# Table activations in earlier gaps, the first row block evacuated in halves, DMA transposes for half of the second batch, and the first cast emitted earlier in a fused retention and Fourier-mix kernel

## The chip, the cores and the metric

One core of a Trainium2 chip. The metric is the device time of one execution in microseconds (us), lower is better. The times are medians of several executions; the profile is of one execution, and its span is a little shorter than the time of the same run (252.5 us of 254.16).

## The reference, cut to what matters

```python
# attention: B, H, S, D = 4, 8, 768, 64; a decaying state per head
state = gamma * state + k[t] (x) v[t]
y[t]  = scale * q[t] @ state
# mix and feed-forward: x = y as [B, S, 512]
mixed = real(fft(fft(x, axis=1), axis=2))
u  = x + mixed
un = (u - mean(u)) / sqrt(var(u) + 1e-6)
out = u + relu(un @ w_ch1) @ w_ch2          # 512 -> 2048 -> 512
```

## The kernel before

Per batch the kernel works on four pairs of heads. A pair's q and k are cast to fp16 (`q16z`, `kd`), transposed (`qTz`, `kT`), multiplied (`wkA`, masked to `atm`), combined with the running state (`s`) to `wkY`, and written to `x`. Then the two Fourier transforms are matmuls with cosine and sine tables: folds `xab` and `eo`, first stage `ps` to `g`, second stage `pq` to `u`. Row blocks `kb` 0 to 5 of 128 rows each are centred (`un`), transposed (`unT`) and fed to the hidden layer `psh` and the output layer `psc`. Batches overlap: while batch b runs its two layers, batch b+1 runs its attention. Only the first batch has nothing to overlap with; this stretch of some 36 us is called the head. `filler(n)` issues n matmuls on zeros whose results nobody reads.

```python
def csn_unit(c):                      # one of the tables; three of them
    nc.scalar.activation(csn[:, c, :], rs[2 * c + 1][:, 0:384], AF.Sin, ...)
...
# end of the first batch's list of units (the head)
un += a(3) + e(3, (0, 0), (1, 0)) + [kv0_unit(3), filler(4), sc_unit(3), t_act(4, 2),
                                     csn_unit(0), csn_unit(1), csn_unit(2)]
un += e(3, (0, 1), (1, 1))
un += [yx_unit(3), yi_unit(3, 0), x0_unit(3, 0), filler(2), yi_unit(3, 1), x0_unit(3, 1), ...]
...
# rows: normalise, then transpose
def norm_unit(b, kb):
    ...
    if b == 0 and kb < 3:
        una = nc.scalar.activation(un, u[:, kb, :], AF.Identity,
                                   bias=fd[0]["mu"][:, kb:kb + 1], scale=-1.0)
...
def unT_unit(b, kb):
    if b >= NPE:                      # NPE = 2: batches 2 and 3 by DMA
        nc.sync.dma_start_transpose(unT[:, :, kb * P:(kb + 1) * P], un)
        return
    for cb in range(4):               # batches 0 and 1 by TensorE
        nc.tensor.transpose(pst[:, cb, :], un[:, cb * P:(cb + 1) * P], ident16)
    ...                               # copied by DVE or ACT
...
# one pair of batches 2 and 3: casts on ACT (q) and POOL (k, v), transposes by DMA
nc.sync.dma_start_transpose(qT..., q16_of[b, i]...)
nc.sync.dma_start_transpose(kT, kd_of[b, i]...)
...
# where each unit is put, in units of a batch; the build then orders every engine's work
streams.append(([load_unit(b + 1, i) for i in range(4)], b + -0.249, b + 0.044))
ts = [0.040, 0.044] + [0.044 + 0.550 * sum(n[:j]) / sum(n) for j in range(6)]
streams.append((steps[0], b + ts[0], b + ts[1]))      # steps[0]: cast and transposes of pair 0
```

Plain loads, output stores and all DMA transposes are issued by one engine, SP, in the order that the build gives them.

## Time and profile before

| | before |
|---|---|
| median time (4 runs) | 254.38 us (254.28 to 254.48) |
| TensorE busy in the profile | 237.9 of 252.5 us |
| start of the dense hidden-layer stream | 41.65 us |
| TensorE idle, 97 to 117 us and 151 to 175 us | 0.85 and 0.81 us |

How to read it: TensorE is the engine with the most work. So outside the head a change is worth what it takes out of TensorE's work or its gaps, and inside the head what it takes out of the chain of waits. The lines stand in the prediction below.

### The profile page before, as it was taken

Reading aid. Unit: us, or ns where it says so; the run is one execution under the profiler, and the core shown is the slowest. Engines: PE = TensorE matmul, PEld = TensorE weight load, DVE = VectorE, ACT = ScalarE, POOL = GpSimd, SP = SyncE. Lnnn points to the kernel's source line nnn. Section 1 sums busy time; section 2 is a strip of 40 time slices with the busy share of each in tenths; the row PEclk is TensorE's granted clock in tenths of the full one; section 3 lists DMA queues with packets and bytes.
Section 4 is the critical chain, followed back from the end, with each engine's and each line's share of the span. In section 5 each row is a group of like instructions: output and inputs, shape, how many; then the busy total and the mean of one; then the engine's idle time right before and its main releaser. Section 6 shows DMA issues by size and latency. Waiting matters only on the chain.

```text
span 252.5 us, 5283 instructions
## 1 busy us (share of the span) xinstructions
PE 237.9 (94%) x2040; PEld 147.7 (59%) x2040; DVE 176.1 (70%) x430; ACT 124.9 (49%) x259; POOL 73.1 (29%) x129
## 2 busy tenths in 40 slices
PE   6798899999999999899999999989999999999994
PEld 2454678856776545566566546755676455545553
DVE  7989857888998786898686727987776545323211
ACT  7878768482674336873245405851156208303400
POOL 6667500494500074480001605720003105000000
PEclk9999999999999999999999999999999999999999
DMA  8999999799999169999999383594100531221012
GB/s 173 262 254 144 194 200 193 166 256 233 287 223 213 48 128 246 179 208 191 241 254 178 73 138 80 97 148 104 56 29 0 65 124 23 44 83 42 1 44 83
DMA packets 97577, 36.00 MB, mean 143 GB/s; under 512 B 88208, under 2 KB 94608, under 8 KB 97552
## 3 DMA queue, kind: packets, MB, share of 16 engines
q1 hardware_dynamic: 93328, 31.47, 62.3%
q0 software_dynamic: 4224, 4.19, 10.4%
q8 instruction: 16, 0.26, 0.4%
q14 instruction: 9, 0.07, 0.1%
HBM read 27.26 MB, written 6.29 MB: 133 GB/s over the span
## 4 chain that ended last, share of the span: by engine, by line
PE 68%; DVE 11%; ACT 7%; DMA 6%; POOL 3%; SPq 2%; issue 2%; ACTq 0%; DVEq 0%
PE psc L900 29%; PE psh L857 21%; PE psh L874 3%; PE ps L687 3%; DMA k<-in_k_dram 2%; PE wkA L568 2%; DMA kT<-kd 2%; DMA qTz<-q16z 2%; SPq L154 2%; DVE atm L570 1%; PE pq L776 1%; PE wkY L621 1%; PE pq L772 1%; ACT un L815 1%; PE wkY L617 1%
## 5 line engine op out<-in xcount | busy, mean ns | idle before, releaser
L900 PE MATMUL psc<-w,ht 128*128 128x512 f16 (+1 forms) x400 | 89.3, 370 | 0.0
L857 PE MATMUL psh<-unT,w 128*128 128x384 f16 x448 | 82.0, 326 | 0.3 <-ACT ht L861 0.3
L900 PEld LDWEIGHTS <-ht 128*128 128x128 f16 x400 | 38.1, 98 | 35.5
L857 PEld LDWEIGHTS <-w 128*128 128x128 f16 x448 | 42.9, 98 | 24.1 <-issue 0.7
L861 ACT ACTIVATE ht<-psh 128x384 f16<-128x384 f32 x73 | 34.4, 489 | 32.2 <-PE psh L857 31.3
L795 POOL TENSOR_TENSOR u<-u,x 128x256 f32<-128x256 f32 x21 | 13.4, 637 | 116.1 <-DVE u L788 111.3
L904 DVE SCALAR_TENSOR_TENSOR ob<-psc,stats,u 128x512 f32<-128x512 f32 (+1 forms) x25 | 18.2, 726 | 26.4 <-PE psc L900 26.4
L863 DVE TENSOR_SCALAR ht<-psh 128x384 f16<-128x384 f32 x39 | 21.4, 552 | 10.1 <-PE psh L857 9.7
L570 DVE TENSOR_TENSOR atm<-wkA,maskp 128x512 f16<-128x512 f32 x36 | 23.7, 684 | 2.1 <-PE wkA L568 2.0
L629 ACT ACTIVATE x<-wkY,gexp 128x384 f16<-128x384 f32 x24 | 12.7, 581 | 20.6 <-PE wkY L621 20.5
L815 ACT ACTIVATE un<-u,stats 128x512 f16<-128x512 f32 x21 | 15.1, 721 | 14.5 <-DVE stats L814 8.6
L813 DVE BATCH_NORM_STATS2 bst<-u 128x6 f32<-128x512 f32 x21 | 14.6, 694 | 10.6 <-POOL u L797 10.5
L785 ACT COPY qn<-pq 128x255 f32<-128x255 f32 x24 | 8.9, 370 | 20.1 <-PE pq L776 19.6
L596 DVE SCALAR_TENSOR_TENSOR s<-s,gkrow,wkK 128x128 f16<-128x128 f16 x48 | 16.3, 340 | 1.2
L140 PE MATMUL wps<-ht 128*128 128x512 f16 x44 | 13.6, 415 | 2.2 <-POOL ht L186 2.2
L568 PE MATMUL wkA<-qTz,kT 128*128 128x256 f16 x72 | 13.1, 273 | 1.7 <-DMA kT<-kd 0.8
L351 POOL TENSOR_SCALAR kd<-k,gexp 128x384 f16<-128x384 f32 x24 | 13.8, 586 | 2.8 <-DMA k<-in_k_dram 2.7
L797 POOL TENSOR_TENSOR u<-u,x 128x256 f32<-128x256 f32 x21 | 13.3, 636 | 2.5 <-DVE u L790 1.3
L788 DVE SCALAR_TENSOR_TENSOR u<-pq,g,qn 128x257 f32<-128x257 f32 x24 | 11.4, 475 | 3.7 <-ACT qn L785 3.6
L874 PE MATMUL psh<-unT,w 128*128 128x128 f16 x192 | 11.4, 219 | 0.4 <-ACT unT L848 0.2
L874 PEld LDWEIGHTS <-w 128*128 128x128 f16 x192 | 11.0, 98 | 0.8 <-issue 0.7
L790 DVE SCALAR_TENSOR_TENSOR u<-pq,g,qn 128x255 f32<-128x255 f32 x24 | 11.3, 469 | 0.0
(142 smaller groups left out, 306.5 us busy)
## 6 DMA issues: line engine op xcount, KB each, us to landing
q<-in_q_dram SPq DMA_DIRECT2D x16, 384.0 KB, 6.3
k<-in_k_dram SPq DMA_DIRECT2D x16, 384.0 KB, 5.7
v<-in_v_dram SPq DMA_DIRECT2D x16, 384.0 KB, 6.1
out_dram<-ob SPq DMA_DIRECT2D x23, 256.0 KB, 2.2
w<-in_moe_w_ch_dram POOLq DMA_DIRECT2D x8, 512.0 KB, 10.9
out_dram<-ob SPq DMA_DIRECT2D x2, 128.0 KB, 1.7
unT<-un SPq DMA_TRANSPOSE x12, 2.5
qTz<-q16z SPq DMA_TRANSPOSE x8, 4.6
```

What stands on the lines that cost most here:

```text
L351: kc = nc.gpsimd.tensor_scalar(out=kd[:, :, h2, :], in0=k32[:, h2], scalar1=gkd[:, h0 + h2:h0 + h2 + 1], scalar2=1.0, op0=ALU.mult, op1=AL ...
L568: nc.tensor.matmul(wk[:, c2], st["kT"][:, c, :], st["qT"][:, :, c, :], start=True, stop=True)
L570: nc.vector.tensor_tensor(out=st["atm"][:, 2 * part:2 * part + 2], in0=wk, in1=maskp[:, PAIR_ORDER[i]].unsqueeze(1).to_broadcast([P, 2, 2, ...
L596: nc.vector.scalar_tensor_tensor(out=s16[:, c], in0=s16[:, c - 1], scalar=gkrow[:, hp, 1:2], in1=wk[:, c - c0], op0=ALU.mult, op1=ALU.add)
L813: nc.vector.bn_stats(bst, u[:, kb, :])
L815: una = nc.scalar.activation(un, u[:, kb, :], AF.Identity, bias=stats[:, kb, 0:1], scale=-1.0)
L857: nc.tensor.matmul(psh, w116[:, cb, fb * P:(fb + 1) * P], unT[:, cb, rt * 384:(rt + 1) * 384], start=(cb == 0), stop=(cb == 3))
L861: nc.scalar.activation(ht16[:, fb, :], psh, AF.Relu, bias=0.0, scale=-1.0)
L863: nc.vector.tensor_scalar(out=ht16[:, fb, :], in0=psh, scalar1=-1.0, scalar2=0.0, op0=ALU.mult, op1=ALU.max)
L874: mm = nc.tensor.matmul(psh[:, f], w116[:, cb, fb * P:(fb + 1) * P], unT[:, cb, kb * P:(kb + 1) * P], start=(cb == 0), stop=(cb == 3))
L900: nc.tensor.matmul(psc[:, c0:c1], ht16[:, fb, rb3 * P:(rb3 + 1) * P], w216[:, fb, c0:c1], start=(fb == 0), stop=(fb == NFB - 1))
L904: nc.vector.scalar_tensor_tensor(out=ob[:, c0:c1], in0=psc[:, c0:c1], scalar=lb[b]["st"][:, rb, 3:4], in1=lb[b]["u"][:, rb, c0:c1], op0=AL ...
```

## The change

The intent has four parts: (1) the three `csn` activations leave the chain for gaps of ACT some 6 to 11 us earlier, and the head's last units change order, with four fillers fewer; (2) the first row block is centred and evacuated in halves; (3) row blocks 3 to 5 of the second batch (b = 1) are transposed by DMA; (4) the first pair of batches 2 and 3 is cast sooner, and their loads are put later. The diff, cut to its core:

```diff
-                una = nc.scalar.activation(un, u[:, kb, :], AF.Identity, ...)
+                for c0, c1 in (((0, 256), (256, DM)) if kb == 0 else ((0, DM),)):
+                    una = nc.scalar.activation(un[:, c0:c1], u[:, kb, c0:c1], AF.Identity, ...)
...
-            if b >= NPE:
+            if b > 1 or b and kb >= 3:
                 nc.sync.dma_start_transpose(unT[:, :, kb * P:(kb + 1) * P], un)
...
+            if b == 0 and kb == 0:
+                nc.scalar.copy(unT[:, 0:2, 0:P], pst[:, 0:2])
+                nc.scalar.copy(unT[:, 2:4, 0:P], pst[:, 2:4])
...
-        un += a(1) + [filler(1), kv0_unit(1)] + ...
+        un += a(1) + [csn_unit(0), filler(1), kv0_unit(1)] + ...
...                          (csn_unit(1) after te_unit(2, 0), csn_unit(2) after t_act(3, 2))
-        un += [fold_s(0, 0, 130, 1, 2), fold_d(0, 0, (0,)), s1_unit(0, 0, 0),
-               fold_s(0, 130, 258, 1, 2), fold_d(0, 0, (1,)), fold_d(0, 1, (0,)), px_unit(0),
-               ...  s1_unit(0, 1, 1), px_unit(1), filler(1), g0_unit(0, (2,)), mean_unit(0)]
-        un += [s2_unit(0, 0), s2_unit(0, 1), norm_unit(0, 0), ..., filler(4), unT_unit(0, 0), ...
+        un += [fold_s(0, 0, 130, 1, 2), fold_d(0, 0), s1_unit(0, 0, 0), fold_s(0, 130, 258, 1, 2),
+               px_unit(0), fold_d(0, 1, (0,)), ... s1_unit(0, 1, 1), g0_unit(0, (2,)),
+               mean_unit(0)]
+        un += [s2_unit(0, 0), px_unit(1), s2_unit(0, 1), norm_unit(0, 0), ..., filler(2), unT_unit(0, 0), ...
...
-    streams.append(([load_unit(b + 1, i) for i in range(4)], b + -0.249, b + 0.044))
+    streams.append(([load_unit(b + 1, i) for i in range(4)], b + -0.249, b + 0.152))
-    ts = [0.040, 0.044] + [...]
+    ts = [-0.040, -0.020] + [...]
```

More of the change, by code (lines that the diff above doesn't have):

```diff
@@ L808, in run @@
             if b == 0 and kb < 3:
-                una = nc.scalar.activation(un, u[:, kb, :], AF.Identity,
-                                           bias=fd[0]["mu"][:, kb:kb + 1], scale=-1.0)
+                for c0, c1 in (((0, 256), (256, DM)) if kb == 0 else ((0, DM),)):
+                    una = nc.scalar.activation(un[:, c0:c1], u[:, kb, c0:c1], AF.Identity,
+                                               bias=fd[0]["mu"][:, kb:kb + 1], scale=-1.0)
                 lb[b]["bst", kb] = bst
@@ L844, in run @@
                 nc.tensor.transpose(pst[:, cb, :], un[:, cb * P:(cb + 1) * P], ident16)
-            if (kb % 2 == 0) != (b == 0 and kb < 3):
+            if b == 0 and kb == 0:
+                nc.scalar.copy(unT[:, 0:2, 0:P], pst[:, 0:2])
+                nc.scalar.copy(unT[:, 2:4, 0:P], pst[:, 2:4])
+            elif (kb % 2 == 0) != (b == 0 and kb < 3):
                 nc.vector.tensor_copy(unT[:, :, kb * P:(kb + 1) * P], pst)
@@ L980, in first_units @@
                                                                      half_ids]
-        un += a(1) + [filler(1), kv0_unit(1)] + e(1, *std) + [sc_unit(1)]
-        un += [q0_unit(2), t0_unit(2, 0), te_unit(2, 0), filler(3), k0_unit(2), t0_unit(2, 1),
-               te_unit(2, 1)]
+        un += a(1) + [csn_unit(0), filler(1), kv0_unit(1)] + e(1, *std) + [sc_unit(1)]
+        un += [q0_unit(2), t0_unit(2, 0), te_unit(2, 0), csn_unit(1), filler(3), k0_unit(2),
+               t0_unit(2, 1), te_unit(2, 1)]
         un += y(1) + [td_dve(0), td_dve(1), yx_unit(1), filler(2)] + x(1) + [
             gk_unit(o[2]), t_act(3, 0), t_act(3, 1), v0_unit(2)]
-        un += a(2) + [filler(1), kv0_unit(2)] + e(2, *std) + [sc_unit(2), t_act(3, 2)]
+        un += a(2) + [filler(1), kv0_unit(2)] + e(2, *std) + [sc_unit(2), t_act(3, 2),
+                                                              csn_unit(2)]
         un += [q0_unit(3), w1_unit(0), t0_unit(3, 0), te_unit(3, 0), filler(3)] + y(2)
@@ L991, in first_units @@
         un += [w1_unit(g) for g in range(1, 4)] + [w2_unit(g) for g in range(4)]
-        un += a(3) + e(3, (0, 0), (1, 0)) + [kv0_unit(3), filler(4), sc_unit(3), t_act(4, 2),
-                                             csn_unit(0), csn_unit(1), csn_unit(2)]
+        un += a(3) + e(3, (0, 0), (1, 0)) + [kv0_unit(3), filler(4), sc_unit(3), t_act(4, 2)]
         un += e(3, (0, 1), (1, 1))
-        un += [yx_unit(3), yi_unit(3, 0), x0_unit(3, 0), filler(2), yi_unit(3, 1), x0_unit(3, 1),
+        un += [yx_unit(3), yi_unit(3, 0), x0_unit(3, 0), filler(1), yi_unit(3, 1), x0_unit(3, 1),
                g0_unit(0, (1,)), filler(1)]
-        un += [fold_s(0, 0, 130, 1, 2), fold_d(0, 0, (0,)), s1_unit(0, 0, 0),
-               fold_s(0, 130, 258, 1, 2), fold_d(0, 0, (1,)), fold_d(0, 1, (0,)), px_unit(0),
-               xmean_unit(0), fold_d(0, 1, (1,)), s1_unit(0, 1, 0), s1_unit(0, 0, 1),
-               s1_unit(0, 1, 1), px_unit(1), filler(1), g0_unit(0, (2,)), mean_unit(0)]
-        un += [s2_unit(0, 0), s2_unit(0, 1), norm_unit(0, 0), gr_unit(0), gr_unit(1),
-               px_unit(2), filler(4), unT_unit(0, 0), xmean_unit(1), mean_unit(1),
+        un += [fold_s(0, 0, 130, 1, 2), fold_d(0, 0), s1_unit(0, 0, 0), fold_s(0, 130, 258, 1, 2),
+               px_unit(0), fold_d(0, 1, (0,)), xmean_unit(0), fold_d(0, 1, (1,)),
+               s1_unit(0, 1, 0), s1_unit(0, 0, 1), s1_unit(0, 1, 1), g0_unit(0, (2,)),
+               mean_unit(0)]
+        un += [s2_unit(0, 0), px_unit(1), s2_unit(0, 1), norm_unit(0, 0), gr_unit(0), gr_unit(1),
+               px_unit(2), filler(2), unT_unit(0, 0), xmean_unit(1), mean_unit(1),
                norm_unit(0, 1), s2_unit(0, 2), xmean_unit(2), mean_unit(2), norm_unit(0, 2),
@@ L1056 @@
             else:
-                streams.append(([load_unit(b + 1, i) for i in range(4)], b + -0.249, b + 0.044))
+                streams.append(([load_unit(b + 1, i) for i in range(4)], b + -0.249, b + 0.152))
                 n = [len(u) for u in steps[1:]]
-                ts = [0.040, 0.044] + [0.044 + 0.550 * sum(n[:j]) / sum(n)
+                ts = [-0.040, -0.020] + [0.044 + 0.550 * sum(n[:j]) / sum(n)
                                          for j in range(6)]
```

## The prediction

> **What bounds the kernel now.** I read the page first, then the busy time by stretch, then TensorE's own order of time, then the chain that ended last, and last the DMA issues. The page says that TensorE (PE) is busy 237.9 of 252.5 us, so the first question is where the other 14.6 us lie. The busy times by stretch answer it (columns: stretch, then the busy us of PE, PEld, DVE, ACT and POOL with instruction counts, the granted clock, the DMA share and GB/s):
>
> ```profile
> 34.00:42.00 8.00, 7.13 (x99) 5.83 (x97) 5.31 (x17) 6.84 (x21) 0.26 (x4) 1.00 1.23 202
> 42.00:62.00 20.00, 20.00 (x225) 14.64 (x223) 16.39 (x41) 11.29 (x21) 10.69 (x17) 1.00 1.02 208
> ...
> 97.00:117.00 20.00, 19.15 (x176) 12.76 (x174) 17.09 (x44) 14.60 (x32) 9.44 (x15) 1.00 1.28 205
> 117.00:141.00 24.00, 24.00 (x202) 15.11 (x200) 18.27 (x42) 9.34 (x20) 2.25 (x4) 1.00 1.06 209
> ...
> 151.00:175.00 24.00, 23.19 (x211) 15.01 (x209) 20.07 (x49) 12.97 (x30) 9.44 (x15) 1.00 0.60 113
> ```
>
> From 42 us on, whole stretches are 100% PE. Asked for 0 to 42 us as one stretch, the same view gives PE 33.94 busy, so 8.06 us idle, and even that includes filler matmuls (44 of them, 13.6 us on the page). The tail after the last matmul, 249.1 to 252.5, is another 3.4 us. That leaves about 3.2 us of PE idle time in the 207 us between. So there are two regimes: a **head of about 36 us that is a chain of waits between engines**, and a **body in which only PE work counts**. The gaps in the body are few, and PE's order of time names the three largest (the bracket is the idle time ahead of the group, and what ended it):
>
> ```profile
> 94.17 0.40 PE L844 MATMUL pst<-ident,un 128*128 128x128 f16 x4 [0.50 <-ACT un L815]
> ...
> 104.95 0.61 PE L568 MATMUL wkA<-qTz,kT 128*128 128x256 f16 x4 [0.85 <-DMA kT<-kd]
> ...
> 169.39 0.38 PE L568 MATMUL wkA<-qTz,kT 128*128 128x256 f16 x2 [0.81 <-DMA qTz<-q16z]
> ```
>
> The second is the first pair of batch 2 waiting for its DMA transpose; the third is a later pair of batch 3. For the head I read the chain in order of time (start, us, what):
>
> ```profile
> 26.26 1.51 ACT csn L270 x3
> 27.77 0.94 ACT x L507 x2
> ...
> 28.74 0.63 DVE xab L646 x2
> 29.37 0.48 DVE eo L656
> ...
> 29.89 1.71 PE ps L687 x18
> ...
> 32.74 0.38 ACT qn L785
> ...
> 33.15 0.49 DVE u L788
> 33.63 0.40 DVE u L790
> ...
> 34.06 0.73 ACT un L809
> ...
> 34.83 0.41 PE pst L844 x4
> ...
> 35.27 0.59 ACT unT L848
> ```
>
> Three table activations (csn) sit between the third pair's work and the last pair's output on ACT, on the chain. The hidden layer's first matmul starts at 35.91, after unT; from there PE is nearly full, so **every us by which 35.91 moves forward should move the end**.
>
> **What the Trainium skill says.** "ScalarE: Activation LUTs", section "What ACT_TABLE_LOAD costs": an ACTIVATE with a per-partition bias costs about 280 ns + 0.833 ns per element, one with immediates 186 ns + 0.833 ns, and neighbours overlap by some 93 ns. The trace agrees: un (512 elements, bias) takes 721 ns against 707, unT (512, copy) 586 against 613, and the three csn on the chain follow each other every 1.51 / 3 = 0.50 us though one lasts 0.60. "TensorE: Matmul & The Clock Gate", Part 1: the clock falls back after an idle window of about 3.4 us. That bears on the fillers that are removed; every stretch here has clock 1.00, and no PE gap after the kernel's first inputs is near 3.4 us. "DMA: Bandwidth & Descriptors", section "Issuing engines are not separate DMA queues": all queues share the same 16 engines, so added transposes compete with the loads. The trace has a DMA share of 1.28 in 97:117 against 0.60 in 151:175, so that is a live risk. "Perfetto Trace Analysis", "Summary: the profiler window per engine type": for such a DMA the recorded span is only the issue, not the movement; I therefore take times to landing.
>
> **Part 1, csn into gaps.** Removed from the chain: 1.51 us. Added: three activations at 0.50 us pitch, each ahead of a copy for which ACT was idle (ACT's order of time):
>
> ```profile
> 15.51 0.80 ACT L415 COPY qTz<-tq 128x768 f16<-128x768 f16 x1 [0.59 <-PE tq L407]
> 17.23 0.80 ACT L418 COPY kT<-tq 128x768 f16<-128x768 f16 x1 [0.92 <-PE tq L407]
> ...
> 21.00 0.80 ACT L415 COPY qTz<-tq 128x768 f16<-128x768 f16 x1 [0.40 <-PE tq L407]
> ```
>
> 0.50 fits in 0.59 and 0.92, and overruns 0.40 by 0.1 at most. So they cost 0 to 0.1 us. The whole 1.51 isn't won, though, because other limits stand right behind it. The last pair's yi matmuls of the first head run at 26.52 to 26.87, so x (L507) can start at 26.9 rather than 27.77 and both are done at about 27.85 rather than 28.71. But DVE is busy without a gap from 25.2 to 28.05: atm ends at about 26.8, then come the fold xab (26.83, 0.62) and eo. In the new order DVE does xab 0.62, two eo of 0.48, xab 0.62, two eo of 0.48 from 26.83 without a wait: 26.83 + 3.2 = 30.03. Before, its last eo ended at 29.37 + 3 x 0.48 = 30.8. The last of the four s1 groups can thus start at about 30.07, not 30.93: **0.85 us**. After it, px of the second row block (4 matmuls, 0.45) and a filler (0.21) leave the place ahead of the s2 matmuls, which before made cd start at 32.10 and sd at 32.33. Now s2 waits only for DVE's last cast g, which ends at about 30.07 + 0.67 + 0.5 = 31.27: sd at 31.3, **1.0 us** earlier in all. Then qn, and u at about 32.1 instead of 33.15.
>
> **Part 2, un and unT in halves.** Before: un 0.73, pst 0.41, unT 0.59 and three hand-overs of about 0.04, from 34.06 to 35.91, 1.85 us. Now the first half of un needs columns 0:256 alone, which the first u instruction (L788) writes, so it can start up to 0.40 us (L790) before the second u ends. The px moved between the two s2 groups delays qn of the second block by 0.45 on ACT, which takes most of that back: ACT would reach the first half at about 32.95. Estimate from the page's formula: a half of un 0.40 pitch, a half of unT 0.31 pitch. Halves of un at 32.95 and 33.35, done by 33.80; PE transposes of the second half until 34.1; copies until about 34.5. The first hidden matmul would start at 34.45, against 35.91. Of this 1.45 I trust 1.0 from part 1 and 0.3 from part 2: **1.3 us** for the head. Fillers are 4 fewer (2 to 1, 1 to 0, 4 to 2), 1.7 us at 0.415 of busy time that lay in waits, so they are worth no time of their own beyond what I have counted.
>
> **Part 3, DMA transposes for row blocks 3 to 5 of the second batch.** 12 PE transposes go. In the stream four of them take 0.22 (the next group starts 0.22 later, as at 110.50 to 110.73): 3 x 0.22 = **0.66 us** of PE, in a stretch where PE is the bound. Two ACT copies of 0.59 and one DVE copy of 0.42 go as well, worth nothing directly (ACT is at 14.6 of 20 us, DVE at 17.1). Three DMA transposes come, median 2.5 us to landing, 1.2 us each on the issuing queue; they feed matmuls that start at about 127 us, and the rows are normalised at 102 to 112, so their own latency is hidden.
>
> **Part 4, first pair cast sooner.** In emission order the casts of pair 0 move by 0.07 to 0.08 of a batch, about 4 us at 54 us per batch. If the transposes follow, kT lands before 104.95 and the 0.85 gap of batch 2 closes. The 0.81 gap of batch 3 belongs to a later pair whose schedule is unchanged; I give it no gain. The loads are emitted up to 0.11 of a batch (5.8 us) later, which only uses slack.
>
> **Sum.** 1.3 + 0.66 + 0.85 = 2.8 us. I charge 0.4 us for new or longer waits (below), so about 2.4 us: 254.34 - 2.4 = 251.9.
>
> **Rivals.** (a) *The issuing queue becomes a wait.* SP issues almost without a pause from 97.6 to 117.5 (transposes of 1.2 to 2.3 us each between loads). Three more fall into that stretch, and kT or qTz of pairs 1 to 3 may land late, as happened in batch 3 (0.81 us), where unT already goes this way. Against it: moving pair 0 forward takes about 3.2 us of issues (1.59 + 1.63) out of it. If it bites, 0.5 to 1.0 us per occurrence, total 252.5 to 253.3. (b) *The early cast blocks ACT.* The two q casts take 0.91 us and ACT works in order; cast too early, they stand ahead of un or unT of batch 1 (93.4 to 95.8), where PE already waits 0.50 at 94.17, or wait for a load. Cost up to 0.9 us, total about 252.8. The gap of 0.49 ahead of unT at 94.61 would hide half. (c) *The head's gain is given back at batch 1's loads.* These wait for the second row block's hidden matmuls and for a weight transfer: of the queue's waits before 45.45, PE psh came last by 2.6 us, so the weights leave 2.6 us of room and a head 1.3 us shorter shifts the loads with it. I hold this unlikely; it would make 253. (d) *Everything works, halves pay fully, and the 0.50 and 0.81 gaps close too*: 1.5 + 0.66 + 2.16 = 4.3, or 250.0, the best that I can construct.
>
> **Range and chances.** The head is worth 0.8 to 1.6, part 3 is 0.5 to 0.66, part 4 with rivals (a) and (b) between +0.9 lost and 1.3 won. That gives 250.8 to 253.2 for 8 times in 10. Faster by over 2% means below 249.25, beyond rival (d): 0.02. Slower by over 2% needs 5 us of new waits: 0.01. Within 2%: 0.97.
>
> **What would show it right or wrong.** Right: no csn on the chain; the last DVE eo before the hidden layer ends near 30.0; first hidden matmul (L874 before) near 34.5; no pst of 102 to 116 us; no wait of wkA for kT at about 104. Wrong: the first hidden matmul at 35 or later, because DVE or qn holds it; PE idle time from 42 to 195 us above the present 2.8 us, with wkA waiting for DMA or psh for ACT; fewer us of the 0.66 because PE is waiting there anyway.

## The result, and the profile after

The changed kernel takes **252.74 us** (252.55 to 253.01, 4 runs) against 254.38 us, 1.64 us less. The ratio is 0.9936, with a 95% interval of 0.9919 to 0.9953. The time is inside the predicted range and "within 2%" came true, but the gain is 0.8 us short of the point of 251.9.

The chain of the changed kernel, in the head (start, us, what):

```profile
27.54 0.57 DVE eo L656
...
28.15 0.69 PE ps L687 x6
28.84 0.44 PE pq L746 x4
29.28 1.69 PE ps L687 x18
...
33.22 0.81 ACT un L810 x2
...
34.40 0.37 ACT unT L847
34.77 0.28 ACT unT L848
35.05 0.63 ACT junk L668 x2
...
35.89 0.72 ACT un L810
...
40.84 6.39 PE psh L878 x112
```

No csn stands there any more, and DVE's folds run without a wait. The first hidden-layer matmul starts at 34.82 instead of 35.91 (1.09 sooner), but the dense stream of 112 hidden matmuls starts at 40.84 instead of 41.65, which is only 0.81 sooner. (One more matmul stands ahead of the stream in the changed kernel; further on, at 93 us, the gain is 0.92.) Between the two the chain is not on TensorE: it runs from unT over ACT's junk (the accumulating copy that gives the second block's mean), the second block's un and qn on ACT, and then DVE's work for the next blocks.

TensorE's order of time in the body (the bracket is the idle time before the group):

```profile
93.25 0.40 PE L845 MATMUL pst<-ident,un 128*128 128x128 f16 x4 [0.50 <-ACT un L816]
115.42 0.38 PE L568 MATMUL wkA<-qTz,kT 128*128 128x256 f16 x2 [0.28 <-ACT x L629]
167.72 0.38 PE L568 MATMUL wkA<-qTz,kT 128*128 128x256 f16 x2 [1.23 <-DMA qTz<-q16z]
```

The wait for kT at 104.95 is gone. A wait of 0.28 at 115.4 is new, and the one in batch 3 has grown from 0.81 to 1.23. The account at one place late in both traces, the hidden group that starts at 214.52 before and at 212.84 after: head 0.92 (93.25 against 94.17, ahead of everything else) + 12 transposes 0.66 + wait gone 0.85 - new wait 0.28 - longer wait 0.42 = 1.73, and the traces differ there by 1.68.

What removed the wait at 104.95 can be read from the SP queue. Before (start, us of the issue, what):

```profile
94.42 0.39 SPq L154 DMA_DIRECT2D k<-in_k_dram  x1
95.08 0.60 SPq L154 DMA_DIRECT2D v<-in_v_dram  x1
97.61 0.36 SPq L908 DMA_DIRECT2D out_dram<-ob  x1
98.08 1.59 SPq L516 DMA_TRANSPOSE qTz<-q16z  x1
99.72 1.63 SPq L518 DMA_TRANSPOSE kT<-kd  x1
```

After:

```profile
93.04 0.36 SPq L912 DMA_DIRECT2D out_dram<-ob  x1
94.16 1.32 SPq L518 DMA_TRANSPOSE kT<-kd  x1
95.53 0.57 SPq L154 DMA_DIRECT2D k<-in_k_dram  x1
96.25 2.64 SPq L516 DMA_TRANSPOSE qTz<-q16z  x1
99.00 0.52 SPq L912 DMA_DIRECT2D out_dram<-ob  x1
```

Before, both transposes stand behind a store (97.61) whose data DVE had only just written (ob, 96.83 to 97.58), though kd was ready at 95.06 and q16z at 96.7. After, they stand ahead of it. The casts themselves have not moved: kd's cast starts at 93.91 before and at 92.98 after, and the 0.93 us between them is the head's gain. What has moved is TensorE's side: the first wkA of batch 2 starts at 100.88 instead of 104.95.

### The profile page after: what moved, and what is told of

The parts are those of the page before. It is cut to its first block, busy times and chain, and to the rows that moved or that the text cites. A ratio compares the mean times of both kernels' runs of the same rounds, so it can differ in the third digit from the quotient of the medians.

```text
span 250.6 us, 5254 instructions
## 1 busy us (share of the span) xinstructions
PE 237.6 (95%) x2024; PEld 146.7 (59%) x2024; DVE 175.5 (70%) x429; ACT 123.6 (49%) x259; POOL 73.0 (29%) x129
## 4 chain that ended last, share of the span: by engine, by line
PE 67%; DVE 10%; ACT 7%; DMA 7%; SPq 3%; POOL 3%; issue 2%; ACTq 0%; DVEq 0%
PE psc L904 28%; PE psh L861 21%; DMA qTz<-q16z 4%; SPq L154 3%; PE ps L687 3%; PE psh L878 3%; DMA k<-in_k_dram 2%; PE wkA L568 2%; ACT un L816 2%; PE pq L776 2%; DVE atm L570 2%; PE pq L772 1%; PE wkY L621 1%; DVE bst L814 1%; ACT x L629 1%
## 5 line engine op out<-in xcount | busy, mean ns | idle before, releaser
L140 PE MATMUL wps<-ht 128*128 128x512 f16 x40 | 12.8, 423 | 2.2 <-POOL ht L186 2.2
```

## The experiments

Twelve kernels ran, each with a profile and five rounds, in three groups; the kernels of a group share the runs of the kernel before, on one chip. All results were correct. A run whose waits matter is read in its trace, because the differences between parts (0.1 to 0.4 us) are as large as the intervals (about 0.3 us to each side). The start of the dense stream is less exact than it looks: the changed kernel and e9 are the same program, yet it starts at 40.84 and 41.07, because the two executions begin their heads 0.23 us apart (the same wkY group of the head at 26.11 and 26.34). Where that matters I subtract the difference of this group. The columns: median, ratio to the kernel before with its interval, start of the dense stream, and TensorE's waits before the first pair's wkA of batch 2, near 115 us, and near 168 us.

| run | us | ratio (95%) | dense | pair 0 | near 115 | near 168 |
|---|---|---|---|---|---|---|
| before (profile shown above) | 254.38 | 1 | 41.65 | 0.85 | none | 0.81 |
| changed | 252.74 | 0.9936 (0.9919 to 0.9953) | 40.84 | none | 0.28 | 1.23 |
| e1 head only | 253.38 | 0.9965 (0.9952 to 0.9977) | 40.79 | 0.74 | none | 0.89 |
| e2 no DMA unT | 252.84 | 0.9943 (0.9930 to 0.9955) | 40.92 | none | none | 1.01 |
| e3 no early cast | 252.93 | 0.9950 (0.9938 to 0.9963) | 40.84 | 0.64 | none | 1.18 |
| e4 transposes late | 253.60 | 0.9967 (0.9953 to 0.9980) | 41.08 | 1.58 | none | 1.27 |
| e5 csn only | 253.65 | 0.9988 (0.9974 to 1.0001) | 41.13 | 0.91 | none | 0.76 |
| e6 no halves | 253.13 | 0.9963 (0.9945 to 0.9981) | 40.85 | none | 0.34 (at 108) | 1.23 |
| e7 mean early | 252.33 | 0.9929 (0.9917 to 0.9941) | 40.70, other order | 0.19 | none | 1.39 |
| e8 row blocks late | 254.50 | 1.0010 (0.9998 to 1.0022) | 40.89 | 0.67 | 0.93 (at 109) | 0.41 (at 163) |
| e9 changed again | 253.00 | 0.9946 (0.9932 to 0.9959) | 41.07 | none | 0.17 | 1.32 |
| e10 two by DMA | 253.25 | 0.9960 (0.9946 to 0.9975) | 40.86 | none | none | 1.40 |
| e11 mean early, three un buffers | 254.59 | 1.0017 (1.0003 to 1.0031) | 40.65, other order | 0.19 | 0.30 (at 109), 0.22 | 1.23 |
| e12 before + DMA unT | 253.97 | 0.9985 (0.9973 to 0.9997) | 41.72 | 0.93 | none | 1.23 |

### e1: the head alone

Parts 1 and 2 on the kernel before: the changed kernel with these lines as they were.

```diff
-            if b > 1 or b and kb >= 3:
+            if b >= NPE:
-    ... b + -0.249, b + 0.152))
+    ... b + -0.249, b + 0.044))
...
-    ts = [-0.040, -0.020] + [...]
+    ts = [0.040, 0.044] + [...]
```

> Parts 1 and 2 alone (the head of the first batch), the rest as before. Theory: the head is worth 0.8 to 0.95 us (the two traces differ by 0.81 us at the start of the dense hidden-layer stream and by 0.92 at 93 us), and nothing of it is given back later, so 254.38 - 0.9 = 253.5 us; the wait of wkA for kT at the first pair of batch 2 (0.85) stays, now near 104.0. Rival: the head's gain is lost at batch 1's loads, then 254.2 or more and new TensorE gaps between 42 and 87 us.

Measured: 253.38 us against 254.26 us of its group, **0.88 us** less. The old wait stays (0.74) and nothing is given back between 42 and 87 us. So the head is worth 0.9 us, and batch 1's loads don't take it back.

### e5 and e6: what of the head does it

e5 is the kernel before with the three `csn_unit` calls moved and nothing else. e6 is the changed kernel without halves:

```diff
-                for c0, c1 in (((0, 256), (256, DM)) if kb == 0 else ((0, DM),)):
+                for c0, c1 in ((0, DM),):
...
-            if b == 0 and kb == 0:
-                ...                  # two half copies
-            elif (kb % 2 == 0) != (b == 0 and kb < 3):
+            if (kb % 2 == 0) != (b == 0 and kb < 3):
```

> The kernel before with nothing but the three csn activations moved into the earlier gaps. Theory: x of the last pair comes 0.8 us sooner, the second fold xab starts as soon as DVE is free (near 28.0 rather than 28.74), and the last eo ends 0.7 sooner, so most of the head's 0.88 us comes from this alone: dense hidden stream (x112) at 40.9 to 41.1, about 253.6. Rival (the new order of eo, px and fillers carries the head): less than 0.4 us, 253.9 or more.

> The changed kernel with un and unT of the first row block whole again. Theory (what follows the first row block on ACT, not the block itself, sets the dense stream): the first hidden matmul comes 0.2 us later, near 35.0, but the dense stream (x112) at 40.9 to 41.05 instead of 40.84, so 252.8 to 252.95. Rival (the halves are worth the 0.3 us of the prediction): 253.05 or more.

Measured: e5's dense stream starts at 41.13 and its median is 0.48 us below its group's 254.13 (one of six runs is an outlier at 254.58, so the interval just reaches 1). The csn move alone gives 0.5 of the head's 0.8 to 0.9 us in the trace, and the new order and the halves the rest; "most of it" was right, and the expected place, 40.9 to 41.1, was missed by 0.03.

e6's time settles nothing: its six runs spread from 252.45 to 254.17, and its trace has an extra wait of 0.34 at 108 us. The head of its trace says more. Chain of e6:

```profile
34.03 0.41 PE pst L845 x4
...
34.46 0.58 ACT unT L849
35.05 0.63 ACT junk L668 x2
...
40.85 6.39 PE psh L875 x112
```

Without halves the first hidden matmul starts at 35.10 instead of 34.82, and yet ACT reaches junk at 35.05 in both kernels, and the dense stream starts at 40.85 in one and 40.84 in the other. But in the changed kernel TensorE has done one matmul more by then (a `pq<-cd,g16r`, which e6 does behind the stream), so the gain has to be read further on, here at the same wkY group, the changed kernel first:

```profile
79.61 0.36 PE L617 MATMUL wkY<-s,qTz 128*128 128x64 f16 x7 [0.23 <-DVE g L694]
```

```profile
79.72 0.36 PE L617 MATMUL wkY<-s,qTz 128*128 128x64 f16 x7 [0.23 <-DVE g L694]
```

The heads of the two executions begin 0.03 us apart (26.11 and 26.08). So **the halves bring the first matmul 0.28 us forward and the work behind it only 0.11 to 0.14 us**. ACT itself gains nothing: its two half un take 0.91 us where one whole took 0.72, and its two half unT 0.65 where one took 0.58, so it comes to junk at the same time, and ACT's next work is what the stream waits for. The longer un is what "ScalarE: Activation LUTs" of the Trainium skill, section "What ACT_TABLE_LOAD costs", leads one to expect: its cost of an ACTIVATE, an estimate, gives 2 x 0.49 - 0.09 = 0.89 for the halves.

### e7: take that wait away

If junk on ACT is what holds the stream, moving it should pay. The second block's mean goes into a gap of ACT ahead of the first s2:

```diff
-    s1_unit(0, 1, 0), s1_unit(0, 0, 1), s1_unit(0, 1, 1), g0_unit(0, (2,)), mean_unit(0)]
+    s1_unit(0, 1, 0), s1_unit(0, 0, 1), xmean_unit(1), s1_unit(0, 1, 1), g0_unit(0, (2,)),
+    mean_unit(0), mean_unit(1)]
-    ... unT_unit(0, 0), xmean_unit(1), mean_unit(1), norm_unit(0, 1), ...
+    ... unT_unit(0, 0), norm_unit(0, 1), ...
```

> The changed kernel with the second row block's mean (the accumulating copy on ACT) moved ahead of the first s2, into an ACT gap of 0.8 us, instead of behind unT. Theory (between first hidden matmul and dense stream 0.28 us were lost because ACT's junk, un, qn chain moved forward by only 0.8): ACT's un of the second block comes 0.6 us sooner, TensorE's idle 0.35 us between 34.8 and 42 shrinks to 0.1, dense stream near 40.6, 252.5. Rival: the activation delays the first u by standing ahead of qn, and nothing or a loss is seen.

Measured: ACT starts the second un at 35.15 instead of 35.89. The groups ahead of the stream are ordered otherwise here, so I compare further on: the wkY group of 0.23 us wait in the body starts at 79.38 against 79.61 in the changed kernel, although this execution began its head 0.21 us later (the same wkY group of the head at 26.32 against 26.11). So the head is 0.44 us shorter. The median, 252.33 us, is the lowest. Its ratio of 0.9929 lies below the changed kernel's 0.9936 and 0.9946 (two groups), but the intervals overlap: the shorter head is shown in the trace, a faster kernel is likely and not shown.

### e3 and e4: what closed the wait of the first pair

e3 undoes part 4. e4 keeps the early casts and puts only the first pair's two transposes back:

```diff
-            streams.append((steps[0], b + ts[0], b + ts[1]))
+            streams.append((steps[0][:1], b + ts[0], b + ts[0] + 0.010))   # cast: early
+            streams.append((steps[0][1:], b + 0.040, b + 0.044))           # transposes: late
```

(for b of 1 and 2; nothing else.) In the built programs e4 differs from the changed kernel by one exchange: SP issues qTz of batch 2's first pair behind the store instead of ahead of it.

> The changed kernel with the casts and loads emitted as before. Theory: the wait for the first pair's transpose at batch 2 comes back, 0.85 us or more, because kT and qTz stand behind an output store in the queue again: about 253.5 us. Rival (the wait was closed by the shorter head or by the removed transposes instead): no gap above 0.3 us near 103 us, and 252.7.

> The changed kernel with the early casts kept, and only the first pair's transposes of later batches emitted late. In the order of instructions a single pair changes places: qTz of batch 2 goes behind the output store instead of ahead of it; the casts stand where they stood. Theory (what closed the wait is the place of the transposes in the queue, not the time of the casts): a wait for qTz of 0.3 to 1 us comes back at the first wkA of batch 2, near 101 us, about 253.2 us. Rival (the casts did it): no wait there and 252.7.

Measured in e4, TensorE's order of time:

```profile
102.78 0.38 PE L568 MATMUL wkA<-qTz,kT 128*128 128x256 f16 x2 [1.58 <-DMA qTz<-q16z]
```

The wait is back, larger than expected, and the time rises to 253.60. With the casts where they were, **the place of one transpose in the issuing queue decides over 1.58 us of TensorE time**. It is not the old wait made larger: in this order TensorE comes to the pair some 3 us sooner than in the kernel before (at 101.20 against 104.10). What the change calls casting sooner works by the order of the queue. In the old order something else lengthens these transposes too: from 101.5 to 103.0 us in the kernel before, while both are under way, the core's DMA moves only 30 GB/s, after 264 before that. e4 has no such hold while its qTz is under way (179 GB/s or more in every us), so its wait is the order's alone; what share the hold had in the old 0.85 is not shown.

In e3 the old order returns with a wait of 0.64. But e3 takes 252.93 us, where 253.5 was expected, a ratio of 0.9950 against 0.9936 and 0.9946 of the changed kernel: part 4 is worth 0.1 to 0.4 us by these values, not 0.85, and with the intervals it may be nothing. The wait near 115 us (0.28) doesn't arise in e3.

### e2, e10, e12: what the added DMA transposes cost

e2 is the changed kernel with `if b >= NPE:` in `unT_unit`, so TensorE transposes all of the second batch. e10 has `kb >= 4` in place of `kb >= 3`. e12 is the kernel before with part 3 alone. e9 is the changed kernel unaltered, in the same group as e10 and e12.

> The changed kernel with the second batch's rows 3 to 5 transposed by TensorE again. Theory: 12 transposes at 0.22 per four come back, +0.66 us, and the 0.28 us gap of wkA at 115.4 us of the changed kernel goes, because that gap comes from unT transposes standing ahead of qTz in the queue: net +0.4, about 253.1. Rival (queue crowding costs more than it saves): equal or faster than the changed kernel, 252.7 or less. Second rival (the added transposes cause the longer wait at 167.7, 1.23 against 0.81): that wait falls back to about 0.8.

> The changed kernel once more, unaltered, as the base of this group and to see whether its waits repeat. Theory: 252.6 to 252.9 us; the wait of wkA near 167.7 at 1.2 to 1.3 us and the 0.28 us at 115.4 again. Rival (the waits are chance of one profile): either of them differs by more than 0.2 us.

> The changed kernel with two instead of three row blocks of the second batch (4 and 5) transposed by DMA; block 3 returns to TensorE (+0.22 us). Theory (the unT of block 3 stands in the queue ahead of qTz and kT and holds a un buffer): the 0.28 us wait at 115.4 goes, so the time is that of the changed kernel within 0.15 us; the late wait at 167.7 stays at 1.2 if any added transpose lengthens it, and is between 0.9 and 1.2 if it grows with their number. Rival (queue crowding has no part in it): +0.22 us with the same waits.

> The kernel before with the second batch's three DMA transposes alone. Theory: TensorE is relieved of 0.66 us, but the wait near 169 us rises from 0.81 to about 1.2 and a wait near 115 of some 0.3 appears, so the gain is 0.1 us or less net: 254.0 to 254.3. Rival (the three waits belong to the other parts): gain of 0.5 us or more, and the wait near 169 stays at 0.8.

Measured: e9 repeats the changed kernel at 253.00 us (0.1 above what was expected), and its waits of 1.32 and 0.17 lie within the 0.2 us allowed. e2 takes 252.84 us, where 253.1 was expected. By the ratios (0.9943 against 0.9936 and 0.9946) part 3 is worth 0.2 us or nothing. e12 says why, in TensorE's order of time:

```profile
105.11 0.61 PE L568 MATMUL wkA<-qTz,kT 128*128 128x256 f16 x4 [0.93 <-DMA kT<-kd]
169.32 0.38 PE L568 MATMUL wkA<-qTz,kT 128*128 128x256 f16 x2 [1.23 <-DMA qTz<-q16z]
```

With the three DMA transposes as the only difference from the kernel before, the wait near 169 goes from 0.81 to 1.23 and that of the first pair from 0.85 to 0.93: 0.66 - 0.42 - 0.08 = 0.16 us should be left. The traces have 0.14 (the hidden group at 214.52 and 214.45, with heads 0.07 apart), and 254.30 to 253.97 is 0.33, with an interval of 0.1 to 0.7. No wait near 115 appears here, so that part of my expectation was wrong.

The wait near 168 sorts all the kernels that keep this stretch's order of instructions. Without DMA transposes in batch 1 it is 0.81, 0.89, 1.01 and 0.76 (before, e1, e2, e5). With them it is 1.23, 1.18, 1.27, 1.23, 1.39, 1.32, 1.40 and 1.23 (changed, e3, e4, e6, e7, e9, e10, e12). The qTz transpose that ends it is issued at the same distance from its cast in both groups; what differs is its own time. Chain of the kernel before, and then of e12:

```profile
164.36 4.90 DMA qTz<-q16z
```

```profile
163.87 5.32 DMA qTz<-q16z
```

From issue to landing it is 4.86 to 5.10 us in the first group and 5.27 to 5.50 in the second, though the added transposes landed 50 us earlier and no loads are under way. That the edit causes it is shown by e12; two transposes instead of three (e10) are no better.

Where in the transfer the time goes can be seen in the DMA rate (`--windows`). In the kernel before, the core's DMA moves 175 GB/s from 164.4 to 166.4 us, but 17 GB/s from 166.7 to 168.0. In e12 it moves 190 GB/s up to 167.2, and then 8 GB/s from 167.6 to 169.0. So the transpose is held for more than a us, in both kernels, and later in e12. In all 13 traces with a transfer of 4.86 us or more, a transfer of 16 KB on the queue that the profile calls "instruction" starts just ahead of the hold. The qTz transposes before and after this one in the kernel before, without either, land in 3.69 and 3.72 us; in e8, where neither falls into this one, it lands in 3.66. The start of that transfer, counted from the issue of qTz, goes with the number of matmuls on the page: 2.00 us in the two kernels with 2040 (before, e5), 2.35 in the two with 2036 (e1, e2), 3.15 to 3.47 in those with 2028 or 2024. So a reading that fits is that taking 12 transposes out of TensorE's program shifts the fetch of its later instructions against the DMA transposes, and not that the queue is crowded. It is not shown: no run moves that transfer alone, and holds of this kind also stand without one (119.6 to 120.9 us in the changed kernel, 21 GB/s).

The wait near 115 is another matter. In the changed kernel's trace ACT idles 1.02 us ahead of a un at 107.8 while the unT transpose of row block 3, which reads the buffer that un will overwrite, is in flight (issued at 105.27, landed at 107.73), and 2.69 us ahead of a q cast at 112.75, until qTz has landed. In e10 block 3 goes back to TensorE and the wait near 115 is gone, as in e2. That does not show the cause: e4, e6 and e7 keep all three DMA transposes and the early cast and don't have this wait either, but others ahead of it (1.58, 0.34 and 0.19). e10 isn't faster for it (253.25 against 253.00, intervals overlapping).

### e8 and e11: attempts to remove the waits, both failed

e8 emits row blocks 3 to 5 later, `(0.004, 0.170, 0.230, 0.371)` for `(0.004, 0.140, 0.200, 0.341)`, so that pair 2's cast stands ahead of the last block's additions on POOL. e11 adds e7's move and a third un buffer to the changed kernel, paid for with one of three store buffers (there was no other room).

> The changed kernel with the mirror row blocks (3 to 5) of later batches emitted later by up to 0.03 of a batch, so that the cast of pair 2 stands ahead of the last block's additions on POOL and its kT and qTz ahead of later unT in the queue. Theory (the wait of 1.23 us at 167.7 comes from the chain addition, kd cast, kT, qTz in order): the wait falls below 0.5 us and so does the 0.28 at 115.4, 251.6 to 252.0. Rival (the transposes themselves are slow and in a row, whatever stands ahead): the wait stays above 0.8 or moves to the next pair, and 252.6.

> A try at a better version: the changed kernel with the second block's mean early (as e7) and three instead of two buffers for un (the store buffers go from three to two to make room). Theory: the head is 0.4 us shorter, ACT no longer waits for an unT transpose to land (1.02 us at 107.8) and the 0.28 us wait at 115.4 goes: 252.0 to 252.2, against 252.7 for the changed kernel. Rival: two store buffers make the output scaling wait for stores, or the order shifts and new waits for kT or qTz take the place: 252.5 or more.

Measured in e8, TensorE's order of time:

```profile
101.20 0.38 PE L568 MATMUL wkA<-qTz,kT 128*128 128x256 f16 x2 [0.67 <-DMA qTz<-q16z]
109.30 0.38 PE L568 MATMUL wkA<-qTz,kT 128*128 128x256 f16 x2 [0.93 <-DMA qTz<-q16z]
163.09 0.38 PE L568 MATMUL wkA<-qTz,kT 128*128 128x256 f16 x2 [0.41 <-DMA qTz<-q16z]
165.06 0.81 PE L861 MATMUL psh<-unT,w 128*128 128x384 f16 x4 [0.73 <-DVE ht L867]
```

The wait of 1.23 is replaced by one of 0.41 and one of 0.73, and batch 2 gets waits of 0.67 and 0.93 that it didn't have: 254.50 us, slower than the changed kernel by almost 2 us. The rival was right: the waits move. e11 takes 254.59 us; its trace has new waits for DVE (0.37 and 0.37 for atm, 0.24 for the output's scaling) and for kT (0.30, 0.22). Buffers and the order changed together here, so it doesn't tell which of them cost the time.

## Why the prediction was right or wrong

The range held; the sum was 0.8 us too good, and two of its terms were mis-sized. That the parts add up in the trace's account (1.73 against 1.68) is in part luck: by the times, taking out part 3 (e2) or part 4 (e3) costs 0.4 us or less each, and the two together are worth 0.5 to 0.7 (e1 against the changed kernel and e9), because each edit also moves other waits.

- **Part 1: right in its mechanism and nearly so in size.** csn fitted: the copy that the third csn could delay began at 21.04 instead of 21.00. The last eo ended at 30.17 (said 30.03), sd started at 31.25 (31.3), u at 32.37 (32.1).
- **Part 2: wrong.** The step that failed is "every us by which 35.91 moves forward should move the end". The first hidden matmul came at 34.82 (34.45 before the discount), but of the 1.09 us only 0.92 are left at 93 us, and of the halves' 0.28 us only 0.11 to 0.14 (e6), where 0.3 was booked. I had read TensorE as nearly full after 35.91 and had not followed ACT past unT, where junk, un and qn of the next block lead the chain. The term "1.3 us for the head" measured 0.88 (e1).
- **Part 3: right on TensorE's work** (no pst from 102 to 116 us), but the wait that it adds in batch 3, 0.42 us, was in no term. I had seen rival (a) in the wrong place: in batch 2's crowded queue, where 0.28 us appeared, and not 50 us later.
- **Part 4: right that the wait would close, wrong in the reason.** "If the transposes follow, kT lands before 104.95" was what happened, but the casts did not move by 4 us; they did not move at all against their neighbours. What keeps the wait closed is the order of SP's queue (e4). Rival (b), the cast blocking ACT in front of un, therefore did not occur. "I give it no gain" for batch 3's wait was too kind: it grew.
- **The charge of 0.4 us for new waits measured 0.70** (0.28 + 0.42). With the head's 1.3 as 0.92, the sum is 1.73, as the traces have it.
- Rival (c), the head given back at the loads, is refuted by e1. Rival (d) needed all gaps to close, and one grew.

## What to carry to other kernels

When work is cut finer to start the next engine sooner, follow the engine that does the cutting: if it ends no sooner, and the next stage waits for its next item, most of the earlier start is lost (0.28 us became 0.11 to 0.14 here). Compare two traces at a place where both have done the same work; a stream's start can hide a matmul that stands ahead of it in one of them. Where several kinds of DMA share one issuing queue, look at what stands ahead of the transfer that an engine waits for: one store ahead of a transpose cost 1.58 us of TensorE time here, with the cast where it was. And when transposes move from a full TensorE to DMA, read the waits for the DMA path again in the whole trace, even in a later batch, before booking the saved matmuls.

## What the Trainium skill lacked or had wrong

- "DMA: Bandwidth & Descriptors", section "Issuing engines are not separate DMA queues", says that the sequencer's time to initiate a DMA "is usually small relative to the DMA itself". For the DMA transposes here the issue took 1.2 to 2.6 us in the changed kernel's first SP lines and in batch 3, against 2.5 us (unT, median) to 4.9 us (qTz, median) from issue to landing. The section does not name the cost that decided here: a transpose queued behind a store (1.58 us of TensorE wait in e4).
- The same page, section "Latency and other measured facts", gives an effective 261 GB/s for a DMA transpose with a non-contiguous middle dimension. A qTz transpose moves 128 x 1536 two-byte elements, 393 KB, in 4.9 us from issue to landing, which is 80 GB/s with all fixed cost, queueing and the hold counted. While transposes move data, the profile counts some 216 GB/s (164.5 to 165.0 us in the kernel before). So the page's figure is not refuted, but the time to landing that an engine waits for can't be had from it.
- No page says that a DMA transpose can be held in mid-transfer: 8 to 17 GB/s for 1.3 to 1.4 us in the kernel before and in e12, and 4.86 to 5.50 us to landing where the qTz before and after it in the kernel before take 3.69 and 3.72.
